# Values by the SyncE queue in fp32 and cast on GpSimd, in a kernel of gated attention and channel mixing

## The chip, the cores and the metric

The kernel runs on one core of one Trainium2 chip. The metric is the device time of a run in microseconds (us), the median of several runs. A core has five engines that run side by side, each with its own program in a fixed order: TensorE (PE in the profile; its weight loads are PEld), VectorE (DVE), ScalarE (ACT), GpSimd (POOL) and SyncE (SP), which only starts transfers here. Engines wait for each other by semaphores. Transfers between the device's memory and the on-chip memory run on 16 DMA engines; here they are started from two queues, that of SyncE (q1 in the profile) and that of GpSimd (q0).

## The reference

Queries, keys and values have 4 batches, 8 heads, 768 positions and 64 columns, in fp32. Keys are cut into 12 blocks of 64. A gate picks for each query the three best blocks by the product with the block's mean key, and its own block; attention is taken over these, causally. The result goes through a token mixing and a channel mixing:

```
k_rep = k.reshape(B, H, n_blocks, block, D).mean(axis=3)
gate_scores = np.einsum('bhsd,bhnd->bhsn', q, k_rep)      # masked causally by block
top_idx = np.argsort(gate_scores, axis=-1)[..., -top_k:]
...
scores = scale * np.matmul(q, k.transpose(0, 1, 3, 2))    # masked by chosen blocks and causally
attn = softmax(scores)
x = np.matmul(attn, v)                                    # heads side by side: 768 x 512 a batch
...
h = np.maximum(xt @ w_tok1, 0.0) @ w_tok2                 # xt: x turned
u = x + h.transpose(0, 2, 1)
out = u + np.maximum(u @ w_ch1, 0.0) @ w_ch2
```

## The kernel before

**The unit of work is a pair of heads**, 16 in all, four to a batch, numbered 0 to 15. For each pair the keys and then the queries are loaded in fp32 as tiles `kl` and `ql` of 128 partitions x 768 (`load_qk`, line 306, issued at line 313 in two halves, one a head, on the SyncE queue). TensorE turns each tile (`transposes`, line 358, names `tkl` and `tql`), ScalarE brings the result out of the accumulation memory (`evac_t`, line 367, `kt` and `qt`), and GpSimd casts it to fp16 head by head (`cast`, line 374, `KA` and `QA`; for pair 0 ScalarE does it). VectorE sums the keys by block (`ksum`, line 387), TensorE multiplies with the queries (`gate`, line 405), VectorE takes the top values (line 463) and makes the mask rows, which are put beside the queries (`put_mask`, line 499), so that the scores (line 513) come out masked. Pairs 0 to 5 are gated one by one, later ones in groups of two or four.

**Attention.** For each of a pair's two heads there are three groups of scores, three exponentials on ScalarE (line 526), for all pairs but the first a multiply of the diagonal blocks with a triangle on VectorE (`diag`, line 533), then 21 matmuls with the values (`av`, line 545) and the division by the sum (lines 553 and 564).

**Values.** The product needs them in fp16, with a column of ones behind the 64, in one of six buffers `V16`. `load_v` (line 316) fetches a pair's values with one transfer from GpSimd's queue (line 320), which casts fp32 to fp16 under way. A buffer can be filled again when the products of six pairs before are done.

**Weights.** Ten transfers on the same GpSimd queue (lines 706 to 711), also cast under way.

**Mixing.** Token mixing (lines 576 to 621) needs a batch's four pairs. Channel mixing (lines 657 and 678) is the larger part of TensorE's work; a batch's channel mixing is spread between the attention of later pairs, and the last is done alone at the end.

**What sets the order.** The kernel writes each engine's program out by hand. Before anything is issued, Python code makes a list of operations (`Op`: engine, time it occupies the engine, time until the result, what it depends on, priority, and for transfers a size) and runs a small model of the chip over it (`plan`, line 109). The model takes at each step the operation that can start soonest, by priority among those that are close; the order that comes out is the order of issue on every engine. SyncE loads are taken strictly by priority (line 155), while stores (kind SPO) go in where they come. `transfers` (line 80) models the two queues: where both have work they share the rate, with 60 to 90% for GpSimd's queue according to the size. Two of its habits matter here:
- A dependence in this list that isn't one of data orders the plan only. On the chip an engine waits for data and buffers, and otherwise for its own turn. The loop at line 831 ties each value load to the query transposes of a pair in this manner.
- Where nothing else is ready in the first 46 us of the plan, TensorE gets stand-in matmuls on a tile `warm` (line 695); their results are not used.

Pair i is prepared at priority `pre`, ahead of its attention at 10 i, by 25 for the first four pairs and by 10 later (with 5 more for groups); its key load has priority `pre - 12` and its query load 0.1 more (line 727). The value load (line 752) has `vpre + 2`.

Of the kernel before, what the change touches and what calls it, by code (L numbers as in the profile page):

```python
# [9 lines left out]
FP = mybir.dt.float32  # L10
# [18 lines left out]
R = 5  # L29
NBN = 4  # L30
# [9 lines left out]
def QACT(i):  # L40
    return i < 1


GATE = {2: 700, 3: 700, 4: 730}
GROUPED = [[0], [1], [2], [3], [4], [5], [6, 7], [8, 9, 10, 11], [12, 13, 14, 15]]
WAIT = [("kt", 3, 1), ("kt", 3, 1), ("qt", 3, 1), ("qt", 3, 1), ("qt", 4, 1), ("qt", 4, 1),
# [172 lines left out]
def kernel(  # L219
# [11 lines left out]
    nc = tc.nc  # L231
    B, H, S, D = q.shape
    NB = S // 64
    NJ = S // 128
# [12 lines left out]

    pairs = [(b, h) for b in range(B) for h in range(0, H, 2)]
    NP = len(pairs)
    RINGS = dict(big=2, bank=3, av=1, ql=3, kl=3, qt=4, kt=2, gs=1, gt=1, gm=1, m8=1, bn=NBN, e0=3, e1=3, e2=3, rc=2,  # L250
                 x16=2, h1=2, u=2, uT=2, h2=1, ob=3)

    def sb(tag, shape, dt, name):
        return sp.tile(shape, dt, tag=tag, bufs=RINGS[tag], name=name)

    def ps(tag, shape, name, dt=FP):
        if tag == "big":
            return pp.tile([128, 1024], FP, tag=tag, bufs=RINGS[tag], name=name)
        return pp.tile(shape, dt, tag=tag, bufs=RINGS[tag], name=name)


    avp = pp.tile([128, 512], FP, tag="av", bufs=1, name="avp")
    V16 = [sp.tile([128, 2, NJ, 65], F16, tag=f"V{r}", name=f"V{r}") for r in range(R + 1)]
# [23 lines left out]
    T = {}  # L287
# [3 lines left out]
    def op(eng, occ, rec, deps, prio, fn, takes=(), size=0):  # L291
        o = Op(eng, occ, rec, deps, prio, fn, takes, size)
        ops.append(o)
        return o

    def pe(occ, deps, prio, fn, takes=(), tail=170):
        return op("PE", occ, occ + tail, deps, prio, fn, takes)

    def act(cols, deps, prio, fn, takes=()):
        return op("ACT", 70 + cols * 0.833, 173 + cols * 0.833, deps, prio, fn, takes)  # L300
# [5 lines left out]
    def load_qk(i, t32, src):  # L306
        b, h = pairs[i]

        def f():
            t = sb(t32, [128, NJ, 2 * D], FP, f"{t32}_{i}")  # L310
            T[t32, i] = t
            for g in range(2):
                nc.sync.dma_start(out=t[:, :, D * g:D * g + D], in_=src[b, h + g].rearrange("(j p) d -> p j d", p=128))  # L313
        return f

    def load_v(i):
        b, h = pairs[i]

        def f():
            nc.gpsimd.dma_start(out=V16[i % (R + 1)].rearrange("p g j d -> p (g j) d")[:, :, 0:D],  # L320
                                in_=v[b, h:h + 2].rearrange("g (j p) d -> p (g j) d", p=128))
        return f


    def load_gate_consts():
        nc.sync.dma_start(out=gown, in_=consts["gown"])
# [25 lines left out]
    def transposes(t32, i):  # L352
        def f():
            p = ps("big", None, f"t{t32}")
            T["tr", t32, i] = p
            t = T[t32, i]
            for j in range(NJ):
                nc.tensor.transpose(out=p[:, 128 * j:128 * j + 128], in_=t[:, j, :], identity=ident32)  # L358
        return f
# [161 lines left out]
    def expo(i, x, g):  # L521
        def f():
            width = GROUPS[g][0]
            e = sp.tile([128, 1024 if g < 2 else 640], F16, tag=f"e{g}", bufs=RINGS[f"e{g}"], name=f"e{g}_{i}_{x}")
            T["e", i, x, g] = e
# [23 lines left out]
    def recip(i, x):  # L549
        def f():  # L550
            rc = sp.tile([128, NJ, 1], FP, tag="rc", bufs=RINGS["rc"], name="rc")
            T["rc", i, x] = rc
            nc.vector.reciprocal(out=rc.rearrange("p n o -> p (n o)"),
                                 in_=T["aps", i, x][:, :, 64:65].rearrange("p n o -> p (n o)"))
# [143 lines left out]
    O = {}  # L698
# [15 lines left out]
    def prepare(i):  # L714
        b, h = pairs[i]
        gi = [n for n, G in enumerate(GROUPED) if i in G][0]
        i0 = GROUPED[gi][0]
        pre = 10.0 * (i0 - (AHEAD if i < FIRST else LATER)) + 2.5 * (i - i0) - (0 if len(GROUPED[gi]) == 1 else EXTRA)
        vpre = 10.0 * (i - (AHEAD if i < FIRST else LATER))
        old = i - R  # L720

        def last_scores(x):
            return [O.get(("sc", old, x, g)) for g in range(3)]

        for t32, src, off in (("kl", k, 0), ("ql", q, 0.1)):
            bf = Buf(t32)
            O[t32, i] = op("SP", 950, 0, [], pre - 12 + off, load_qk(i, t32, src), [bf], size=1750)
            big = Buf("big")
            O["tr", t32, i] = pe(660, [O[t32, i]], pre + off, transposes(t32, i), [big], tail=320)
            bf.users.append(O["tr", t32, i])  # L730
            name = "kt" if t32 == "kl" else "qt"
            tb = Buf(name)
            O[name, i] = act(768, [O["tr", t32, i]],
                             pre + 0.5 + off, evac_t(t32, i), [tb])
            big.users.append(O[name, i])
            dst = KA if name == "kt" else QA
            for x in range(2):
                occ = 770
                if QACT(i):
                    O["cast", name, i, x] = act(768, [O[name, i]] + last_scores(x), pre + 0.9 + 0.2 * x + off, cast_act(dst, name, i, x))  # L740
                    tb.users.append(O["cast", name, i, x])
                    continue
                O["cast", name, i, x] = op("POOL", occ, occ + 55, [O[name, i]] + last_scores(x), pre + 4 + off,
                                           cast(dst, name, i, x))
                tb.users.append(O["cast", name, i, x])
            if name == "kt":
                O["ksum", i] = dve(870, [O["kt", i]], pre + 1, ksum(i))
                tb.users.append(O["ksum", i])
                O["kcopy", i] = dve(200, [O["ksum", i], O.get(("gate", old))], pre + 1, kcopy(i))
            else:  # L750
                qb = tb
        O["v", i] = op("POOL", 1060, 0, [O.get(("av", i - R - 1, x)) for x in range(2)], vpre + 2, load_v(i), size=1350)
        n = len(GROUPED[gi])
        O["qb", i] = qb
        if i == GROUPED[gi][-1]:
            G = GROUPED[gi]
            if n == 1:
                gb = Buf("bank")
                O["gate", i] = gate_op = pe(1120, [O["kcopy", i], O["qt", i]], pre + 2, gate(i), [gb])
            else:  # L760
                tbig = Buf("big")
                gate_op = pe(GATE[n], [O["kcopy", m] for m in G] + [O["qt", m] for m in G], pre + 2, gate_t(gi), [tbig])
                for m in G:
                    O["gate", m] = gate_op
                gtb = Buf("gt")
                ge = act(S - 128, [gate_op], pre + 2.1, gate_e(gi), [gtb])
                tbig.users.append(ge)
                gb = Buf("big")
                gback = pe(550, [ge], pre + 2.2, gate_b(gi), [gb])
                gtb.users.append(gback)  # L770
            for m in G:
                O["qb", m].users.append(gate_op)
            gs = Buf("gs")
            O["gm", gi] = dve(75 + 125 * n, [gate_op] if n == 1 else [gback, own_op], pre + 3, gm(gi), [gs])
            gb.users.append(O["gm", gi])
            tops = [dve(720, [O["gm", gi]], pre + 3, top(gi, s)) if s == 0 else None for s in range(n)]
            for s in range(1, n):
                tops[s] = dve(720, [tops[0]], pre + 3, top(gi, s))
            O["lt", gi] = dve(75 + 125 * n, tops, pre + 3, below(gi))
            O["bias", gi] = dve((75 + 125 * n) if n == 4 else 200 * n, [O["lt", gi], O.get(("mask", gi - NBN))] + ([own_op] if n == 4 else []), pre + 3, bias(gi))  # L780
            gs.users += [O["bias", gi]]
            O["lt", gi].two = O["bias", gi].two = True
            mb = Buf("bank")
            O["mask", gi] = pe(280, [O["bias", gi]], pre + 4, mask(gi), [mb])
            for s, m in enumerate(G):
                for x in range(2):
                    O["put", m, x] = dve(410, [O["mask", gi]] + [O.get(("sc", m - R, x, g)) for g in range(3)],
                                         pre + 4, put_mask(gi, s, x))
                    mb.users.append(O["put", m, x])
# [38 lines left out]
        for i in G:  # L828
            attend(i)

    for i, d in enumerate((1, 2, 2, 3, 3, 4, 4, 5, 6, 7, 8, 9, 10, 11, 12, 13)):
        O["v", i].deps.append(O["tr", "ql", d])
    own_op.deps.append(O["cast", "qt", 4, 1])
    for x in range(2):
        O["cast", "kt", 0, x].deps.append(O["qt", 0])
# [80 lines left out]
    kernel_plan.update(ops=O)  # L916
    order, span = plan(ops, RINGS)

# [65 lines left out]
```

The softmax here doesn't subtract the row's maximum and nothing guards it: scores larger than these inputs give would overflow.

## Time and profile before

| | |
|---|---|
| time, median of 3 runs | 266.84 us (266.03 to 267.7) |
| span of the profiled run | 265.2 us |
| TensorE clock granted | 0.998 |
| key loads: 32 transfers of 192 KB, issue to landing | 5.8 us median |
| query loads: 32 transfers of 192 KB | 5.5 us |
| value loads: 16 transfers of 192 KB (fp16 as written) | 8.3 us |
| weight loads: 8 of 384 KB for the channel mixing | 12.2 us |
| packets' time on q1 (SyncE), share of 16 engines | 38.6% for 21.33 MB |
| packets' time on q0 (GpSimd), share of 16 engines | 27.1% for 7.08 MB |

How to read the lines further on. In a table by stage each row has the stretch and its length in us, then the busy time and number of instructions of each engine, the granted clock, the DMA share (it can go over 1, since packets of two queues overlap on an engine) and GB/s. In a group of instructions the columns are the line, the engine, the operation, the tiles written and read, their shapes, the count, the busy time in us, the mean in ns, and the idle time of the engine ahead of them with what ended it. In the list of waits a row gives who waited, for whom, the sum in us, how many times, and sometimes the longest. In the list in order of time and in the chain of waits the first two numbers are the start and the length in us; a bracket at the end is the idle time just before. A busy TensorE isn't TensorE at its peak, because the ends of its instructions are modelled.

### The profile page before, as it was taken

What the parts mean: (1) busy time and instruction counts of PE and PEld (TensorE: products, weight loads), DVE (VectorE), ACT (ScalarE), POOL (GpSimd) and SP (SyncE); (2) the same over time, 40 slices, a digit from 0 to 9 for tenths busy, and PEclk for the clock granted to TensorE, in tenths of its full rate; (3) what the DMA queues carried; (4) which work ended last, traced back from release to release, by engine and by line L of the source; (5) the groups of instructions that cost most, each with busy time, mean ns of one, the idle gap of its engine ahead of it and who ended that gap; (6) DMA issues with size and microseconds to landing.
All of it is one profiled execution on the core that took longest, in us unless ns stands there. A gap on an engine that the chain in (4) does not pass through costs nothing.

```text
span 265.2 us, 5842 instructions
## 1 busy us (share of the span) xinstructions
PE 256.0 (97%) x2304; PEld 166.3 (63%) x2304; DVE 158.9 (60%) x536; ACT 145.3 (55%) x195; POOL 79.9 (30%) x112
## 2 busy tenths in 40 slices
PE   7889999999997999999999999999999999999994
PEld 7877888895765767455666566655455544456443
DVE  4668869896976569986557975493243253333222
ACT  3757898677796966458873699860034400044000
POOL 8494819849446645225420000000000000000000
PEclk9999999999999999999999999999999999999999
DMA  8999999999996999059511000009220025310032
GB/s 169 203 189 197 173 179 208 196 187 194 192 155 134 210 205 159 36 60 174 69 45 41 1 2 0 2 0 189 90 79 2 0 48 150 121 40 0 2 141 97
DMA packets 91322, 28.77 MB, mean 109 GB/s; under 512 B 84896, under 2 KB 87840, under 8 KB 91296
## 3 DMA queue, kind: packets, MB, share of 16 engines
q1 hardware_dynamic: 63232, 21.33, 38.6%
q0 software_dynamic: 28064, 7.08, 27.1%
q8 instruction: 18, 0.29, 0.5%
q14 instruction: 8, 0.07, 0.1%
HBM read 26.83 MB, written 6.29 MB: 125 GB/s over the span
## 4 chain that ended last, share of the span: by engine, by line
PE 84%; DVE 7%; SPq 2%; DMA 2%; ACT 1%; issue 1%; POOL 1%; DVEq 0%; ACTq 0%
PE c L657 23%; PE c L678 23%; PE sps L513 13%; PE avp L545 7%; PE ups L588 3%; PE tql L358 3%; PE tkl L358 2%; SPq L313 2%; DMA kl<-in_k_dram 2%; PE tok L576 2%; PE gps L405 2%; DVE m L463 1%; DVE kst L387 1%; PE gtp L415 1%; DVE QA L499 1%; PE tok L607 1%
## 5 line engine op out<-in xcount | busy, mean ns | idle before, releaser
L526 ACT ACTIVATE e<-sps 128x1024 f16<-128x1024 f32 (+1 forms) x96 | 84.3, 920 | 17.5 <-PE sps L513 14.0
L657 PE MATMUL c<-uT,wc 128*128 128x256 f16 (+1 forms) x384 | 69.1, 326 | 0.0
L678 PE MATMUL c<-wc,h 128*128 128x512 f16 (+2 forms) x300 | 65.6, 370 | 0.0
L667 ACT ACTIVATE h<-c 128x512 f16<-128x512 f32 x48 | 28.7, 598 | 61.1 <-PE c L657 42.9
L657 PEld LDWEIGHTS <-wc 128*128 128x128 f16 x384 | 36.5, 98 | 23.0 <-issue 0.2
L513 PE MATMUL sps<-QA,KA 88*128 88x512 f16 (+3 forms) x256 | 50.1, 305 | 0.0
L678 PEld LDWEIGHTS <-h 128*128 128x128 f16 x300 | 28.7, 98 | 30.6 <-issue 1.0
L533 DVE TENSOR_TENSOR e<-e,m 128x256 f16<-128x256 f16 x90 | 29.7, 337 | 14.5 <-ACT e L526 13.9
L374 POOL CAST KA<-kt 64x768 f16<-64x768 f32 x30 | 24.6, 821 | 45.1 <-ACT kt L367 28.0
L669 DVE TENSOR_SCALAR h<-c 128x256 f16<-128x256 f32 x48 | 20.3, 422 | 26.8 <-PE c L657 26.4
L686 DVE TENSOR_TENSOR ob<-u,c 128x512 f32<-128x512 f16 (+2 forms) x25 | 16.5, 664 | 32.2 <-PE c L678 32.1
L513 PEld LDWEIGHTS <-KA 88*128 88x128 f16 x256 | 23.1, 99 | 17.0 <-issue 0.7
L374 POOL CAST QA<-qt 64x768 f16<-64x768 f32 x30 | 25.5, 850 | 6.5 <-ACT qt L367 5.1
L545 PEld LDWEIGHTS <-e 128*128 128x128 f16 x672 | 25.4, 97 | 2.8
L545 PE MATMUL avp<-V,e 128*128 128x65 f16 x672 | 26.7, 193 | 0.0
L367 ACT COPY kt<-tkl 128x768 f32<-128x768 f32 x16 | 12.8, 798 | 12.8 <-PE tkl L358 7.2
L387 DVE TENSOR_REDUCE kst<-kt 128x12 f32<-128x768 f32 x16 | 15.2, 950 | 6.3 <-ACT kt L367 6.0
L564 DVE TENSOR_TENSOR x<-avp,rc 128x384 f16<-128x384 f32 x32 | 17.8, 555 | 0.8
L320 POOL DMA_DIRECT2D V<-in_v_dram x16 | 16.5, 1033 | 5.6 <-PE avp L545 3.4
L367 ACT COPY qt<-tql 128x768 f32<-128x768 f32 x16 | 12.8, 801 | 5.0 <-PE tql L358 5.0
L499 DVE COPY QA<-bps 24x640 f16<-24x640 f16 x32 | 14.3, 480 | 2.1 <-PE bps L493 1.8
L358 PE MATMUL tkl<-id,kl 128*128 128x128 f32 x96 | 13.6, 277 | 1.9 <-DMA kl<-in_k_dram 1.9
(66 smaller groups left out, 212.5 us busy)
## 6 DMA issues: line engine op xcount, KB each, us to landing
kl<-in_k_dram SPq DMA_DIRECT2D x32, 192.0 KB, 5.8
ql<-in_q_dram SPq DMA_DIRECT2D x32, 192.0 KB, 5.5
out_dram<-ob SPq DMA_DIRECT2D x23, 256.0 KB, 2.0
V<-in_v_dram POOLq DMA_DIRECT2D x16, 192.0 KB, 8.3
wc<-in_moe_w_ch_dram POOLq DMA_DIRECT2D x8, 384.0 KB, 12.2
w<-in_moe_w_tok_dram POOLq DMA_DIRECT2D x2, 384.0 KB, 9.8
out_dram<-ob SPq DMA_DIRECT2D x1, 160.0 KB, 1.8
out_dram<-ob SPq DMA_DIRECT2D x1, 96.0 KB, 1.7
```

Source lines behind the costliest of these rows:

```text
L358: nc.tensor.transpose(out=p[:, 128 * j:128 * j + 128], in_=t[:, j, :], identity=ident32)
L367: nc.scalar.copy(out=t, in_=p[:, 0:S])
L374: nc.gpsimd.tensor_copy(out=to, in_=src)
L387: nc.vector.tensor_reduce(out=kst, in_=kt.rearrange("p (n w) -> p n w", w=64), axis=AX.X, op=ALU.add)
L513: nc.tensor.matmul(out=p[:, off + a:off + a + n], lhsT=KA[i % R][x][0:MK, 128 * kk:128 * kk + 128], rhs=QA[i % R][x][0:MK, q0 + a:q0 + a + ...
L526: nc.scalar.activation(out=e[:, 0:width], in_=T["sps", i, x, g][:, 0:width], func=AF.Exp, scale=scale)
L533: nc.vector.tensor_tensor(out=d, in0=d, in1=m0.rearrange("p (a b) -> p a b", a=1).broadcast_to([128, 2, 128]), op=ALU.mult)
L545: nc.tensor.matmul(out=p[:, jq, :], lhsT=T["e", i, x, g][:, o:o + 128], rhs=V16[i % (R + 1)][:, x, kk, :], start=(kk == 0), stop=(kk == jq))
L657: nc.tensor.matmul(out=p, lhsT=wc1_16[:, cc, 128 * fc:128 * fc + 128], rhs=T["uT", b][:, cc, a // 128:e // 128, :], start=(cc == 0), stop= ...
L667: nc.scalar.activation(out=T["h2", b][:, fc, a:e], in_=T["c1", b, fc, n], func=AF.Relu)
L669: nc.vector.tensor_scalar(out=T["h2", b][:, fc, a:e], in0=T["c1", b, fc, n], scalar1=0.0, scalar2=None, op0=ALU.max)
L678: nc.tensor.matmul(out=T["c2", b, j, lo], lhsT=T["h2", b][:, fc, 128 * j:128 * j + 128], rhs=wc2_16[:, fc, lo:hi], start=(fc == 0), stop=( ...
```

## The change

Values no longer come through GpSimd's queue with a cast under way. They are loaded as fp32 by the SyncE queue into one of two new buffers `v32` (128 x 768 fp32), and GpSimd casts them from there into `V16` with an instruction. Where the loads stand among the key and query loads is written out in a list `VAT`, one priority for each pair: the values of pair 0 after the queries of pair 1, those of pair 1 after the queries of pair 2, those of 2 and 3 after the queries of pair 3, those of 4 and 5 after the queries of the same pair, 6 and 7 together after the queries of 7, and from pair 8 on each behind the queries of its pair. The cast stands in GpSimd's plan where the load stood, and waits for the load and for the products that free the buffer; a `v32` buffer is free again when its cast is done. The loop that tied the value loads to query transposes goes. What is left on GpSimd's queue is the ten weight loads. It is meant to keep the values from competing with keys and queries at times that the plan doesn't know, and to take them off the queue on which the weights wait.

```diff
+VAT = [-26.8, -16.8, -6.9, -6.8, 18.2, 28.2, 36.0, 36.1, 53.2, 55.7, 58.2, 60.7, 93.2, 95.7, 98.2, 100.7]
...
-    RINGS = dict(big=2, bank=3, av=1, ql=3, kl=3, qt=4, kt=2, gs=1, gt=1, gm=1, m8=1, bn=NBN, e0=3, e1=3, e2=3, rc=2,
+    RINGS = dict(big=2, bank=3, av=1, ql=3, kl=3, qt=4, kt=2, v32=2, gs=1, gt=1, gm=1, m8=1, bn=NBN, e0=3, e1=3, e2=3, rc=2,
                  x16=2, h1=2, u=2, uT=2, h2=1, ob=3)
...
         b, h = pairs[i]
 
         def f():
-            nc.gpsimd.dma_start(out=V16[i % (R + 1)].rearrange("p g j d -> p (g j) d")[:, :, 0:D],
-                                in_=v[b, h:h + 2].rearrange("g (j p) d -> p (g j) d", p=128))
-        return f
-
+            t = sb("v32", [128, 2 * NJ, D], FP, f"v32_{i}")
+            T["v32", i] = t
+            nc.sync.dma_start(out=t, in_=v[b, h:h + 2].rearrange("g (j p) d -> p (g j) d", p=128))
+        return f
+
+    def cast_v(i):
+        return lambda: nc.gpsimd.tensor_copy(out=V16[i % (R + 1)].rearrange("p g j d -> p (g j) d")[:, :, 0:D], in_=T["v32", i])
...
-        O["v", i] = op("POOL", 1060, 0, [O.get(("av", i - R - 1, x)) for x in range(2)], vpre + 2, load_v(i), size=1350)
+        vb = Buf("v32")
+        load = op("SP", 700, 0, [], VAT[i], load_v(i), [vb], size=1750)
+        O["v", i] = op("POOL", 820, 870, [load] + [O.get(("av", i - R - 1, x)) for x in range(2)], vpre + 2, cast_v(i))
+        vb.users.append(O["v", i])
...
-    for i, d in enumerate((1, 2, 2, 3, 3, 4, 4, 5, 6, 7, 8, 9, 10, 11, 12, 13)):
-        O["v", i].deps.append(O["tr", "ql", d])
     own_op.deps.append(O["cast", "qt", 4, 1])
```

## The prediction

> **What bounds the kernel now.** I read the totals of the page first, then the table by stage, then the stand-in matmuls alone, then the waits of TensorE, and last the chain and the groups. Totals, busy us and share of the span:
>
> ```profile
> PE 256.0 (97%) x2304; PEld 166.3 (63%) x2304; DVE 158.9 (60%) x536; ACT 145.3 (55%) x195; POOL 79.9 (30%) x112
> ```
>
> TensorE is the bound, with GpSimd (POOL) far from it. So an edit is worth only what it takes out of TensorE's time without useful work. The stages (length, then busy us and count of TensorE, its weight loads, VectorE, ScalarE and GpSimd, clock, DMA share, GB/s):
>
> ```profile
> 5.00:35.00 30.00, 28.02 (x350) 23.51 (x349) 21.08 (x88) 22.24 (x28) 19.71 (x24) 1.00 1.39 194
> 35.00:80.00 45.00, 44.77 (x547) 34.83 (x546) 37.33 (x138) 36.04 (x49) 28.66 (x38) 1.00 1.41 186
> 80.00:86.00 6.00, 4.25 (x48) 3.28 (x47) 4.02 (x10) 3.72 (x5) 4.46 (x6) 1.00 0.67 134
> 86.00:146.00 60.00, 59.52 (x554) 37.36 (x553) 43.63 (x176) 39.72 (x51) 23.04 (x27) 1.00 0.66 111
> ```
>
> The same table for line 695 alone, the stand-in matmuls that are issued where nothing else is ready:
>
> ```profile
> 5.00:35.00 30.00, 7.41 (x102) 6.26 (x102) 1.00 1.39 194
> 35.00:80.00 45.00, 0.00 (x0) 0.00 (x0) 1.00 1.41 186
> ```
>
> From 5 to 35 us TensorE idles 1.98 us and runs 102 stand-ins. The chain has 15 of them in 0.80 us, 0.053 us each; their busy time overlaps, so they cost 102 x 0.053 = 5.4 us. After 35 us there are none: the channel mixing of an earlier batch fills every gap. Idle time after that is 0.23, 1.75 and 0.48 us in the three stages. All that any edit of the loads can win is about 5.4 + 2.0 + 2.5 = 9.9 us, of which 7.4 lies before 35 us.
>
> Where the idle time lies, and the start of the chain:
>
> ```profile
> PE tkl L358 <- DMA kl<-in_k_dram: 1.9, 3, 1.1
> 82.22 0.84 PE L358 MATMUL tkl<-id,kl 128*128 128x128 f32 x6 [0.61 <-DMA kl<-in_k_dram]
> 85.50 0.85 PE L358 MATMUL tql<-id,ql 128*128 128x128 f32 x6 [1.14 <-ACT h L667]
> ...
> 7.63 5.70 DMA kl<-in_k_dram
> 13.33 0.14 issue
> 13.47 0.85 PE tkl L358 x6
> ```
>
> Two places count. At 13.47 the transposes of the third key tile come 1.07 us late. Behind them, in TensorE's fixed order, stand the first scores (14.15), though their mask rows were written by 12.89. At 82 to 86 us two transposes wait, 0.61 and 1.14 us; the second is put down to ScalarE, but as scores and output use other buffers I read it as the query load that follows in the queue.
>
> ```profile
> L320 POOL DMA_DIRECT2D V<-in_v_dram x16 | 16.5, 1033 | 5.6 <-PE avp L545 3.4 <-PE sps L513 2.2
> L374 POOL CAST QA<-qt 64x768 f16<-64x768 f32 x30 | 25.5, 850 | 6.5 <-ACT qt L367 5.1
> L533 DVE TENSOR_TENSOR e<-e,m 128x256 f16<-128x256 f16 x90 | 29.7, 337 | 14.5 <-ACT e L526 13.9
> 6.99 1.18 POOL L320 DMA_DIRECT2D V<-in_v_dram  x1
> ```
>
> The first of these is what is removed, the second prices what is added, the third is who can be disturbed, and the last is the cause of the late key tile: the first value load starts at 6.99. The planner is told to hold it until the query transposes of pair 1 (10.32), but that is an entry in its list and no wait on the chip, so the load runs 3.3 us sooner than the order was made for.
>
> **What the skill says.** (1) "DMA: Bandwidth & Descriptors", section "Issuing engines are not separate DMA queues": all queues share the same 16 engines, and changing queue saves only issue time. The trace agrees on the sharing: with no value load under way, a key or query tile of 1536 packets took 1.7 to 1.9 us from first packet to last; the tile of 9.1 to 12.4 us, beside the first value load (9.8 to 13.3), took 3.3. (2) Same page, "SWDGE vs HWDGE vs iDMA": a cast inside a DMA is only to be had from GpSimd's queue; so the move forces the cast instruction. (3) "SBUF — State Buffer", "Who interferes with whom": a VectorE instruction with two SBUF inputs contends with a GpSimd instruction that reads SBUF. The trace agrees: of the 90 diagonal multiplies (line 533), 19 overlap a GpSimd cast or copy and take 527 ns in the mean, 71 do not and take 287.
>
> **The change, part by part.**
>
> *GpSimd.* Removed: 16 issues x 1.033 = 16.5 us. Added: 16 casts of 128x768. No row shows 128 partitions; a 64x768 cast takes 0.821 to 0.850, and a 24x768 copy of line 333 takes 0.818, so the number of partitions hardly matters: 16 x 0.83 = 13.3 us (if it scaled with partitions, 26). Net -3.2 us on an engine that is 30% busy: worth nothing by itself. But a DMA issue did not read SBUF and a cast does: casts and copies on GpSimd go from 69 to 85. By proportion 19 x 16/69 = 4.4 more multiplies overlap, x 0.24 us = 1.1 us of VectorE, spread over 16 pairs while VectorE is 70 to 83% busy. I charge 0.3 us, between 0 (filled by other work) and 1.1.
>
> *The transfers.* From the packet records: a value load is 1536 packets of 32 ns on GpSimd's queue against 18 ns (alone) to 24 ns (contended) for the same 256 source bytes on the SyncE queue. Over 16 engines that is 3.1 against 1.7 to 2.3 us per load; for the 12 loads ahead of 85 us, 9 to 16 us of engine time less. Against it: with both queues active the engines overlap them (shares of 1.4 above), so part of that saving was never wall time. Over 28 to 84 us GpSimd's queue never ran dry, because values stood among the weights, and key and query tiles took up to 7 to 8 us each. With only 10 weight loads there (22.7 us of engine time) I estimate the eleventh key tile 3 to 4 us earlier. That removes most of the waits at 82 to 86: -1.4 of 1.75 us.
>
> *The first tiles.* The SyncE order becomes keys and queries of pairs 0 and 1, values 0, keys and queries 2, values 1, then pair 3. Queries 1 end at 9.2. Values 0 then take 9.2 to 11.0, keys 2 11.0 to 12.8, plus the 1.0 us seen between last packet and start of the transposes (12.4 to 13.47): 13.8 against 13.47. Queries 2: 15.6, as now. Keys 3 at about 19.3 are used at 22.4 now, so nothing waits. What changes is the order: the planner now has values 0 ahead of keys 2 on one queue, as the chip will, so the first scores (ready at about 13.0) need not stand behind a late transpose. Scores at about 13.1 instead of 14.15, and the gate of pair 1 (16.31 now, its sums ready at 14.24, standing behind the queries' transposes) up to 1.5 us sooner. ScalarE, near 100% busy from 26 to 37 us, starts its exponentials that much sooner, and stand-ins vanish by as much: -1.5 us, between +0.4 (same order, tile later) and -3.
>
> *New waits.* Each value load waits for one of two fp32 buffers, so for the cast two pairs earlier; behind it on SyncE stand the next keys. Load 7 waits for cast 5, load 10 for cast 8, load 12 for cast 10 (now those value loads are issued at 40.4, 58.2 and 66.9). SyncE in turn issues the key and query tiles next to them at about 46, 75 and 87 us, so each buffer is free by then: 0 for the forecast. The output stores stand behind all of it on SyncE, but begin at 111 us. A cast of values waits for the product five to six pairs back, as the load did (3.4 us once): same place in GpSimd's order, no new cost. Small gaps elsewhere (0.23 + 0.48): -0.4 with loads earlier.
>
> Sum: 0.3 - 1.4 - 1.5 - 0.4 = -3.0; 266.8 - 3.0 = 263.8 us.
>
> **Rivals.** A, *the start moves more*: of the 7.4 us without work before 35 us up to 4 vanish, since with queue and plan agreeing all orders up to pair 3 fit: 1.4 + 4 + 0.4 = 5.8, 261 us. For: 5.4 us of stand-ins; against: ScalarE 22.2 of 30 and VectorE 21.1 of 30 us busy there, so other chains close up. B, *hidden anyway*: the order at the start stays, keys 2 are 0.3 us later, the waits at 82 us go in part but VectorE's 0.3 to 1.1 us come back: 266.2. For: TensorE is filled after 35 us whatever the loads do. C, *the SyncE queue jams*: a value load waits for its buffer while keys stand behind it, or 16 more loads on one queue no longer overlap with the second. Keys of pairs 8 to 11 then come 3 to 6 us late, and with the wait of 82 us grown by that: 270. For: SyncE already takes up to 7 us for one tile's two issues at 68 us; against: the buffer dates above.
>
> **How the numbers follow.** Forecast 0.40, A 0.18, B 0.24, C 0.18. Over 1% faster is below 264.2: three quarters of the forecast case and A, 0.30 + 0.18 = 0.48. Within 1%: the rest of the forecast and B, 0.34. Slower: C, 0.18. The range from 260.0 to 268.0 holds the forecast and B, nearly all of A and the mild part of C.
>
> **What would show it.** Right: value packets at 18 to 24 ns; casts at about 0.83 us; the first scores before 13.5 us and before the third key transposes; fewer than 102 stand-ins; no idle stretch of TensorE over 0.5 us at 80 to 86; overlapped multiplies in the low twenties. Wrong: SyncE idle on a GpSimd cast with late key transposes behind it; stand-ins unchanged or more; casts near 1.6 us; idle TensorE time at a new place between 40 and 110 us.

## The result, and the profile after

The changed kernel takes 276.49 us (median of 4 runs, 274.1 to 278.36) beside 267.27 us of the kernel before (4 runs, 266.03 to 267.71): a ratio of 1.0323, with an interval of 1.0238 to 1.0408. It is 9.2 us slower by the medians (8.6 us without the run of 278.36 us, which was of a slower kind and is left out of the ratio), where 3.0 us less were forecast. The profiled execution has a span of 275.0 us.

The totals of the page after (busy us, share of the span, instructions):

```profile
PE 261.0 (95%) x2328; PEld 169.2 (62%) x2328; DVE 162.8 (59%) x536; ACT 145.5 (53%) x195; POOL 77.3 (28%) x112
```

TensorE is busy for 5 us more although its work is the same, and GpSimd for 2.6 us less, as planned. The table by stage says where (length, then busy us and count of TensorE, weight loads, VectorE, ScalarE, GpSimd, clock, DMA share, GB/s):

```profile
5.00:35.00 30.00, 28.28 (x366) 24.20 (x366) 20.50 (x85) 21.01 (x26) 18.83 (x24) 1.00 1.15 210
35.00:80.00 45.00, 37.81 (x431) 29.38 (x427) 29.69 (x93) 27.78 (x38) 26.84 (x37) 0.89 1.09 200
80.00:86.00 6.00, 6.00 (x62) 4.04 (x60) 5.51 (x35) 4.64 (x7) 0.83 (x1) 1.00 1.11 219
86.00:146.00 60.00, 59.60 (x567) 38.23 (x566) 46.68 (x144) 43.15 (x55) 26.83 (x32) 1.00 0.64 131
```

The loss lies in the second stage. Before, TensorE idled there for 0.23 us and ran 547 matmuls at full clock; now it idles for 7.19 us, runs 431, and the mean clock is 0.89. The other stages are as full as before or fuller. Which waits these are is seen in TensorE's timeline from 58 to 75 us (start, us, in brackets the idle time before and what ended it):

```profile
58.94 0.83 PE L625 MATMUL ups<-h,w 128*128 128x128 f16 x12
...
62.64 1.05 PE L362 MATMUL tql<-id,ql 128*128 128x128 f32 x6 [2.87 <-DMA ql<-in_q_dram]
67.66 1.51 PE L362 MATMUL tkl<-id,kl 128*128 128x128 f32 x6 [3.96 <-DMA kl<-in_k_dram]
...
70.89 1.91 PE L661 MATMUL c<-uT,wc 128*128 128x512 f16 x4
```

TensorE stands still for 2.87 us for the queries of pair 7 and for 3.96 us for the keys of pair 8. From 63.1 to 73.3 us its clock is at half, and the transposes between the waits take 1.05 to 1.51 us instead of 0.85. The chain of waits at that place leads to the load of the keys and from there to SyncE's queue:

```profile
59.79 3.37 SPq L314
63.16 0.05 issue
63.21 4.31 DMA kl<-in_k_dram
67.52 0.14 issue
67.66 1.51 PE tkl L362 x6
```

I give the landing of a load as the trace has it, in us, and beside it the time at which the kernel's own planner expected it when it wrote the order down.

| tile | landed before | landed after | the plan after expected |
|---|---|---|---|
| queries 2 | 15.49 | 16.64 | |
| queries 3 | 20.03 | 24.56 | |
| queries 6 | 45.26 | 53.94 | |
| keys 7 | 49.74 | 55.57 | |
| queries 7 | 56.91 | 62.51 | 49.3 |
| keys 8 | 62.25 | 67.52 | 52.4 |
| queries 8 | 67.74 | 69.31 | |
| keys 9 | 74.59 | 72.83 | |
| keys 10 | 82.09 | 82.68 | |

From queries 6 to keys 8 the tiles come 5 to 9 us later than before, and queries 7 and keys 8 come 13 and 15 us later than planned. Both columns turn out to matter. In the kernel before, keys 8 were planned for 51.8 us and also came late, at 62.2 us, but the order used them only at a planned 66.5 us, on the chip at 69.93 and without a wait (TensorE's timeline of the kernel before):

```profile
69.93 0.87 PE L358 MATMUL tkl<-id,kl 128*128 128x128 f32 x6
```

The order of the changed kernel uses them at a planned 57.4 us.

Why they come late is seen in the queues. From 36 to 60 us, the DMA view of each kernel (packets, MB written, time of their packets as a share of 16 engines), first before:

```profile
q0 software_dynamic: 7281, 2.92, 97.6%
q1 hardware_dynamic: 6477, 1.62, 44.4%
```

and after:

```profile
q0 software_dynamic: 1399, 2.47, 59.6%
q1 hardware_dynamic: 8222, 2.07, 43.2%
```

q1 is SyncE's queue, q0 GpSimd's. A key, query or value load is 1536 packets. Counted in such loads, SyncE's queue moved 4.1 of them before while 4.0 value loads went through GpSimd's queue among the weights: 8.1 in 24 us. After, SyncE's queue has to take all three kinds and moves 5.2. Its packets are cheaper than those of the casting loads were (21 ns in the mean over the whole kernel, against 32), but it gets no larger part of the engines. Where no weights run, the same queue moves 0.50 to 0.55 loads per us; beside the weights it moves 0.22, about 40%.

Counted in bytes written, nothing was lost: the two lines give 4.54 MB in the 24 us before and 4.54 MB after, and over the whole second stage the tables have 186 and 200 GB/s. But a value load that is cast under way writes 192 KB, and one in fp32 384 KB. At 0.19 MB per us the eight value loads of pairs 0 to 7 would then take about 8 us more (an estimate from these figures), which is near the 5 to 9 us above. Whether the limit is in bytes written or in how the queues share the engines isn't separated by any run here.

SyncE's own timeline shows it held up (start, us, issues):

```profile
32.22 11.46 SPq L314 DMA_DIRECT2D kl<-in_k_dram  x2
43.78 2.07 SPq L314 DMA_DIRECT2D ql<-in_q_dram  x2
```

The two issues of one key tile, that of pair 6, hold SyncE for 11.46 us, 8.47 of them for the first half. Its buffer had been free since the transposes of keys 3 (they start at 21.81), so I read this as a full queue; no run tests that reading.

The parts of the change itself, from the groups and the issues of the page after:

```profile
L327 POOL CAST V<-v 128x768 f16<-128x768 f32 x16 | 13.4, 835 | 30.9 <-DMA v<-in_v_dram 19.7
L537 DVE TENSOR_TENSOR e<-e,m 128x256 f16<-128x256 f16 x90 | 32.4, 371 | 14.4 <-ACT e L530 13.6
v<-in_v_dram SPq DMA_DIRECT2D x16, 384.0 KB, 5.6
```

A cast takes 835 ns, and GpSimd stands idle for 19.7 us ahead of casts whose values have not landed. The diagonal multiplies cost 2.7 us more than before.

### The profile page after: what moved, and what is told of

Read it like the earlier page. It is cut to its first block, busy times and chain, and to the rows that moved or that the text cites. A ratio compares the mean times of both kernels' runs of the same rounds, so it can differ in the third digit from the quotient of the medians.

```text
span 275.0 us, 5913 instructions
## 1 busy us (share of the span) xinstructions
PE 261.0 (95%) x2328; PEld 169.2 (62%) x2328; DVE 162.8 (59%) x536; ACT 145.5 (53%) x195; POOL 77.3 (28%) x112
## 4 chain that ended last, share of the span: by engine, by line
PE 80%; DVE 6%; DMA 5%; SPq 5%; issue 1%; ACT 1%; DVEq 0%; ACTq 0%
PE c L661 23%; PE c L682 22%; PE sps L517 12%; PE avp L549 7%; SPq L314 4%; DMA ql<-in_q_dram 4%; PE tql L362 3%; PE ups L592 2%; PE tkl L362 2%; PE tok L580 2%; DMA kl<-in_k_dram 2%; PE gtp L419 1%; DVE QA L503 1%; PE gps L409 1%; DVE m L467 1%
## 5 line engine op out<-in xcount | busy, mean ns | idle before, releaser
L661 PE MATMUL c<-uT,wc 128*128 128x256 f16 (+1 forms) x384 | 69.3, 328 | 0.0
L537 DVE TENSOR_TENSOR e<-e,m 128x256 f16<-128x256 f16 x90 | 32.4, 371 | 14.4 <-ACT e L530 13.6
L517 PEld LDWEIGHTS <-KA 88*128 88x128 f16 x256 | 22.4, 98 | 18.1 <-issue 2.7
L327 POOL CAST V<-v 128x768 f16<-128x768 f32 x16 | 13.4, 835 | 30.9 <-DMA v<-in_v_dram 19.7
L362 PE MATMUL tql<-id,ql 128*128 128x128 f32 x96 | 14.3, 288 | 4.2 <-DMA ql<-in_q_dram 4.2
L362 PE MATMUL tkl<-id,kl 128*128 128x128 f32 x96 | 14.2, 287 | 4.0 <-DMA kl<-in_k_dram 4.0
```

The costliest lines, as they stand in the source:

```text
L517: nc.tensor.matmul(out=p[:, off + a:off + a + n], lhsT=KA[i % R][x][0:MK, 128 * kk:128 * kk + 128], rhs=QA[i % R][x][0:MK, q0 + a:q0 + a + ...
L537: nc.vector.tensor_tensor(out=d, in0=d, in1=m0.rearrange("p (a b) -> p a b", a=1).broadcast_to([128, 2, 128]), op=ALU.mult)
L661: nc.tensor.matmul(out=p, lhsT=wc1_16[:, cc, 128 * fc:128 * fc + 128], rhs=T["uT", b][:, cc, a // 128:e // 128, :], start=(cc == 0), stop= ...
```

## The experiments

Two theories stood at the start. Theory 1: the 16 value loads in SyncE's queue delay the keys and queries. Theory 2: the casts on GpSimd do it, through VectorE or through what waits behind them. A third came up as the runs went on: the order that the planner wrote is made for landings that don't happen. The ratios are to the kernel before, on the same chip.

**e1: the loads of values 4 to 7 left out**.

```
 def f():                                  # load_v
+    if 4 <= i < 8:
+        T["v32", i] = T["v32", i - 2]
+        return
```

> The changed kernel with its order kept and the transfers of the values of pairs 4 to 7 left out (their casts read the buffers of pairs 2 and 3 again). Theory 1 (the values stand in SyncE's queue among keys and queries, and while the weights run on the other queue this one gets the smaller part): queries 7 and keys 8 arrive at least 7 us sooner, both waits of TensorE (2.87 and 3.96 us at 60 to 68 us) and the clock drop after them go: 264 to 268 us. Theory 2 (the casts on GpSimd and their contention with VectorE cost the time): the casts are all still there, so 274 to 277 us.

268.68 us, ratio 1.0097 (1.0062 to 1.0131): some 2.4 us are left of the loss, as the kernel before took 266.3 us beside it, with all casts in place. Queries 7 land at 53.40 and keys 8 at 55.99. TensorE's waits by releaser (us, number, longest):

```profile
PE tql L365 <- DMA ql<-in_q_dram: 1.7, 2, 1.1
PE tkl L365 <- DMA kl<-in_k_dram: 0.8, 1, 0.8
```

against 4.2 and 4.0 us of the changed kernel. So four transfers in that queue are enough for most of the loss. One thing more changes: casts that needn't wait let the last two weight loads start at 62.4 instead of 69.3 us.

**e2: the casts of values 6 to 15 left out**, with the loads kept.

```
 def cast_v(i):
+    if i >= 6:
+        return lambda: None
```

> The changed kernel with its order kept and the ten casts of values of pairs 6 to 15 left out (the products use the values of earlier pairs), all transfers kept. Theory 1 (SyncE's queue): the waits for queries 7 and keys 8 stay within 0.5 us of 2.87 and 3.96, 273 to 277 us. Theory 2 (casts): 8.3 us of GpSimd and the waits on it fall away, 266 to 271 us.

280.29 us, ratio 1.0535 (1.0492 to 1.0579): slower than the changed kernel, which neither theory had. TensorE's timeline:

```profile
67.73 1.52 PE L364 MATMUL tkl<-id,kl 128*128 128x128 f32 x6 [7.36 <-DMA kl<-in_k_dram]
```

One wait of 7.36 us stands in place of the two of 2.87 and 3.96 us: queries 7 land at 57.00 here, and keys 8 at 67.59, as in the changed kernel. What comes later than there are queries 8 (72.30 against 69.31, with a wait of 2.55 us) and keys 9 (75.72 against 72.83). The reason stands on GpSimd. Its issue of the last two weight loads, in the timeline of GpSimd in e2:

```profile
61.97 1.52 POOL L717 DMA_DIRECT2D wc<-in_moe_w_ch_dram  x2
```

and in the changed kernel:

```profile
69.34 1.52 POOL L715 DMA_DIRECT2D wc<-in_moe_w_ch_dram  x2
```

Without casts that wait for values, these loads start 7.4 us sooner, and then queries 8 and the end of keys 8 travel beside them. So leaving the casts out wins nothing, and the waiting casts had even held the competition back. As the weights moved with them, this alone doesn't clear the casts; e1 and e5, with all casts in place and little or no loss, do, and theory 2 falls. The price that theory 1 had left out is the weights beside the queue.

**e3: 50 and 70 stand-ins ahead of the two late transposes**, to keep the clock up.

```
+ahead = {id(O["tr", "ql", 7]): 50, id(O["tr", "kl", 8]): 70}
 for o in order:
+    for n in range(ahead.get(id(o), 0)):
+        dummy(n)()
```

> The changed kernel with 50 stand-in matmuls ahead of the transposes of queries 7 and 70 ahead of those of keys 8, in the time in which TensorE waits (about 2.7 and 3.8 us of stand-ins). If the clock drop to about half at 64 to 73 us comes from TensorE having stood still: clock stays at 1.0, and the time falls by 2.5 to 3.5 us to 272.5 to 274. If the drop has another cause: 276 to 277 us.

276.57 us, ratio 1.0363 (1.0291 to 1.0435), the same as the changed kernel. One stretch of 5 us, first of the changed kernel:

```profile
65.00:70.00 5.00, 2.34 (x14) 2.31 (x15) 0.15 (x1) 0.66 (x1) 3.85 (x5) 0.50 1.16 223
```

then of e3:

```profile
65.00:70.00 5.00, 3.45 (x55) 3.27 (x53) 1.71 (x7) 0.80 (x1) 4.49 (x6) 1.00 0.92 200
```

And TensorE's timeline of e3 after that:

```profile
69.78 0.85 PE L362 MATMUL tql<-id,ql 128*128 128x128 f32 x6 [1.55 <-DMA ql<-in_q_dram]
74.87 0.85 PE L362 MATMUL tkl<-id,kl 128*128 128x128 f32 x6 [2.23 <-DMA kl<-in_k_dram]
```

The clock stays at 1.00 and nothing is won: faster work arrives sooner at the next late load and waits there. The test isn't quite clean, since queries 7 landed at 56.27 in this execution, so that the first 50 stand-ins filled a wait that wasn't there; keys 8 landed at 66.91, about as the 70 stand-ins ended. I had counted the slow clock as part of the loss; it is a sign of the wait, and the landings set the time.

**e4: the loads of values 6 and 7 moved behind queries 8**, the rest of the order kept.

```
+late = [O["vload", 6], O["vload", 7]]
+order = [o for o in order if o not in late]
+at = order.index(O["ql", 8]) + 1
+order[at:at] = late
```

> The changed kernel with the loads of values 6 and 7 moved on SyncE from before keys 8 to behind queries 8, every other order kept. Theory 1: keys 8 land two loads, about 3.6 us, sooner, the wait for them falls from 3.96 to under 0.8 us, the wait for queries 7 stays at 2.9, the clock drop is shorter: 270 to 273 us, unless the casts of values 6 and 7, now later, hold up the query casts behind them by as much. Theory 2 (casts): no change, 275 to 278 us.

278.52 us, ratio 1.0468 (1.0429 to 1.0507); missed. Keys 8 land at 64.27, 3.3 us sooner, but the waits only move:

```profile
64.36 1.51 PE L362 MATMUL tkl<-id,kl 128*128 128x128 f32 x6 [3.73 <-DMA kl<-in_k_dram]
...
74.04 1.51 PE L362 MATMUL tkl<-id,kl 128*128 128x128 f32 x6 [3.01 <-DMA kl<-in_k_dram]
```

Values 6 and 7 now stand ahead of keys 9, which land at 73.91 instead of 72.83. GpSimd stands idle for 12.22 us for the values of pair 6 and issues the last weights at 72.5, and these run beside keys 10 (landed at 83.08).

**e5: the planner keeps the backlog.** The planner models the queues' rates, but two of its lines drop every transfer that was due over 2 us ago. With the transfer goes the work it leaves in the queue, so later loads are believed early. Without these lines it plans the changed kernel anew:

```
 for o, d in transfers(moves).items():
     done[id(o)] = max(done.get(id(o), 0.0), d)
-now = min(free.values())
-moves = [(a, o) for a, o in moves if done[id(o)] > now - 2000]
```

> The changed kernel with one line of the planner taken out: the one that forgets transfers already due to be done, so that the plan loses the queue's backlog. Its plan then has keys 8 landing at 72.7 us instead of 52.4 (on the chip 67.5), and all orders are made anew from that. Theory 1a (the transfers are slow, but it is TensorE's fixed order, made for loads 13 to 15 us earlier, that turns this into waits): TensorE's waits for loads fall below 1 us in all, 264 to 269 us. Theory 1b (between 47 and 75 us there is nothing else to do than wait for the loads, whatever the order): the idle time comes back as stand-ins or other waits, 273 to 278 us.

267.25 us (20 runs), ratio 1.0025 (1.0004 to 1.0047). The loss is gone, with all 16 loads and casts in place and, up to 90 us, SyncE's issues in the same order as in the changed kernel. TensorE's waits for loads in e5:

```profile
PE tql L360 <- DMA ql<-in_q_dram: 1.1, 2, 0.7
```

and its second stage:

```profile
35.00:80.00 45.00, 43.70 (x514) 33.13 (x514) 35.39 (x129) 32.97 (x46) 24.19 (x34) 1.00 1.06 204
```

The transfers are about as slow as in the changed kernel: keys 8 land at 68.37, later than there, and 26 loads are through SyncE's queue at 68 us in both. But now the plan expects keys 8 at 72.7, and TensorE does other work first. In its timeline the queries of pair 7 and the keys of pair 8 are turned without a wait:

```profile
66.20 0.82 PE L360 MATMUL tql<-id,ql 128*128 128x128 f32 x6
...
75.74 0.82 PE L360 MATMUL tkl<-id,kl 128*128 128x128 f32 x6
```

The new plan also moves weight loads (two start at 56.9 instead of 53.2, the last two at 64.7 instead of 69.3), and queries 7 land at 57.39 instead of 62.51. That isn't what removes their wait: at 66.20 the landing of the changed kernel would have been in time too. So the slow queue alone costs nothing here; it costs when the order of the work counts on a fast one.

**e6: the last four weight loads later.** In the changed kernel they move on GpSimd behind the query cast of pair 9; **e7** does the same to the kernel before.

```
+late = W[6:10]
+order = [o for o in order if o not in late]
+at = order.index(O["cast", "qt", 9, 1]) + 1
+order[at:at] = late
```

> The changed kernel with every order kept but one: the four loads of the second channel weights on GpSimd come after the query cast of pair 9 (about 88 us) instead of at 53 and 69 us; nothing needs them before 110 us. Theory 1: without a second queue SyncE's queue runs at its full rate of a load in 1.8 us from 53 us on; queries 7 land 2 to 3 us sooner, keys 8 about 6 us sooner; the waits of 2.87 and 3.96 us fall below 1.5 us in all: 265 to 270 us. If the queue were slow by itself: the same waits, 274 to 278 us.

> The kernel before, with the same four weight loads moved behind the query cast of pair 9 (about 85 us) and nothing else. If keys and queries of pairs 7 to 11 are late there for the same reason: keys 10 land before 80 us, the waits of 0.6 and 1.1 us at 82 to 86 go, 263.5 to 265.5 us. If values on GpSimd's queue were the larger part: no change, 266 to 267 us.

e6: 273.41 us, ratio 1.0196 (1.0129 to 1.0263): about 3 us of the 9.2, less than I expected, and with an interval that overlaps that of the changed kernel. With the weights away, queries 7 land at 57.29 and keys 8 at 62.67, 4.9 us sooner, and TensorE waits 2.60 us for the latter, since the order still counts on 52.4. That the weights slow SyncE's queue is shown by the landings; moving them away isn't enough. e7: 274.4 us, ratio 1.0247 (1.0181 to 1.0312), where I expected no harm. The weights, now at 86.8 to 100.8 us, travel beside the tiles of pairs 13 and 14; queries 14 land at 107.74, and an order that was made without that waits:

```profile
107.87 1.51 PE L358 MATMUL tql<-id,ql 128*128 128x128 f32 x6 [3.36 <-DMA ql<-in_q_dram]
```

So the kernel before, too, is sensitive to a transfer that comes later than its order assumes.

**e8: values 0 to 3 alone by SyncE**, all others as before with their ties; planned with the two lines.

```
+def ON_SP(i):
+    return i < 4
```

> Half of the change: values of pairs 0 to 3 by SyncE with a cast, those of 4 to 15 by GpSimd's queue as before, tied in the plan as before. Theory 1: by 28 us both kernels have moved equally many loads, and no weights run before 30 us, so this half costs little: 265 to 269 us. Rival (the early values delay keys 2 and 3, and the delay is carried to the end): 270 to 274 us.

275.76 us, ratio 1.0304 (1.0226 to 1.0381); missed, the loss is nearly whole. The wait is of the same kind as in the changed kernel, though values 6 and 7 aren't in SyncE's queue:

```profile
65.10 1.51 PE L372 MATMUL tkl<-id,kl 128*128 128x128 f32 x6 [4.00 <-DMA kl<-in_k_dram]
```

So it isn't a matter of which values are in the queue at 50 us. Each new plan places its order anew against landings that it believes too early.

**e9: the kernel before, with the planner's two lines out** (edit as e5).

> The kernel before with the same planner line taken out as in the fifth experiment, values on GpSimd's queue. If both ways of loading values are about equal once the plan knows the backlog: 265 to 268 us, like the changed kernel with that line out (267.25). If the move itself costs something that the better plan only hid: 261 to 264.5 us here. If the old plan's optimism did the kernel before good: 269 us or more.

267.33 us (20 runs), ratio 1.0011 (0.9981 to 1.0042). The second stage:

```profile
35.00:80.00 45.00, 43.82 (x533) 33.66 (x529) 34.80 (x127) 32.57 (x46) 25.88 (x35) 1.00 1.30 189
```

With a plan that keeps the backlog, values through GpSimd's queue give 267.33 us and values through SyncE's 267.25 us, with ratios of 1.0025 and 1.0011 whose intervals overlap. The way that the values take is worth nothing that 20 runs can tell.

**e10: the kernel before with the lines out and a hopeful share of rates; e11: the changed kernel with the same.** With both queues at work the two now get 1.2 of the rate together.

```
-SHARE = ((3000.0, 0.8), (2000.0, 0.9), (0.0, 0.6))
+SHARE = ((3000.0, 0.85), (2000.0, 0.85), (0.0, 0.6))
...
-rate[False] = 1.0 - rate[True]
+rate[False] = 1.2 - rate[True]
```

> The kernel before with the planner's line out and its sharing set nearer to what the traces show (weights 0.85 of the rate, the other queue 0.35 beside them, so that two queues together move 1.2). Plan and chip then differ less for keys of pairs 7 to 11: waits for loads below 1 us, 263 to 266 us; if such waits weren't what bounds it: 266 to 268 us.

> The changed kernel with the planner's line out and the same sharing (0.85, 0.35). In the fifth experiment loads landed 4 to 10 us before the plan thought at 44 to 70 us; with this they should agree within 4 us. Theory 1a: no waits for loads over 1 us, 265 to 267.5 us. If that plan is now too hopeful again, keys 8 are waited for and the time is 270 us or more.

e10: 274.94 us, ratio 1.0252 (1.0167 to 1.0337); missed. An order that is too hopeful harms the kernel before in the way the change did:

```profile
62.93 1.20 PE L356 MATMUL tkl<-id,kl 128*128 128x128 f32 x6 [4.46 <-DMA kl<-in_k_dram]
```

e11: 270.48 us, ratio 1.0122 (1.0065 to 1.0178), with four waits for queries of 3.2 us in all. That is less lost than in e10 and more than in e5.

**e12: values 8 to 15 alone by SyncE, planned as e10; e15: the same values, planned as e5.**

```
+def ON_SP(i):
+    return i >= 8
```

> Values of pairs 8 to 15 by SyncE with a cast, those of 0 to 7 by GpSimd's queue as before, with the planner's line out and the sharing 0.85 and 0.35. While the weights run, values then stand in the favoured queue, and later on the even one. Theory 1: loads up to 60 us as in the kernel before, no waits over 1 us, 262.5 to 265.5 us, faster than both. If the gain is eaten by the eight casts or a new order: 266 to 269 us.

> Values of pairs 8 to 15 by SyncE with a cast, the others by GpSimd's queue, and the planner's line out with its sharing as it was (the pessimistic one, which did well in the fifth and ninth experiments). The twelfth experiment had the hopeful sharing and waited 8.7 us for one query tile. If hope in the plan was the trouble: no wait over 1.2 us, 263 to 268 us. If values by SyncE from pair 8 on are the trouble: 272 us or more.

e12: 273.77 to 279.69 us in four runs, too far apart for a ratio. e15: 268.5 us (8 runs), ratio 1.0077 (1.0035 to 1.0119). The longest wait of e12, in a run of 277.97 us:

```profile
69.35 1.51 PE L370 MATMUL tql<-id,ql 128*128 128x128 f32 x6 [8.72 <-DMA ql<-in_q_dram]
```

and those of e15:

```profile
PE tkl L370 <- DMA kl<-in_k_dram: 1.5, 2, 1.1
```

The same transfers with two plans are at least 3 us apart (273.77 is the quickest run of e12, 270.81 the slowest of e15). No mixture beats the kernel before.

**e13: the changed kernel, transfers in the same order on both queues, only the compute reordered by hand.** The transposes of queries 7, keys 8, queries 8 and keys 9, and what hangs on them, stand behind about 4.3 us of channel mixing.

```
+move = [("tr", "ql", 7), ("tr", "kl", 8), ("tr", "ql", 8), ("tr", "kl", 9), ...]
+at = order.index(O["ch1", 0, 2, 0]) + 1
+order[at:at] = move
```

> The changed kernel with its transfers in the same order on both queues. Only on TensorE, and with it on ScalarE, VectorE and GpSimd, the transposes of queries 7, keys 8, queries 8 and keys 9 and what hangs on them are put behind 4.3 us of channel mixing, scores, masks and products (about 4.6 us of work) that the plan had behind them. If the order makes the loss: this work fills as much of the 6.8 us of waits, less after-effects, 269 to 273 us. If the slow transfers make it, whatever the order: 275 to 278 us.

273.26 us, ratio 1.0257 (1.0231 to 1.0283), just above the range that I gave for the order. All four runs are quicker than the quickest of the changed kernel (273.96 against 274.1), and the median is 3.2 us lower, but the intervals of the ratios overlap, so how much the order alone won isn't settled. The waits:

```profile
PE tkl L362 <- DMA kl<-in_k_dram: 2.3, 2, 1.7
PE sps L517 <- DVE QA L503: 1.0, 1, 1.0
PE tql L362 <- DMA ql<-in_q_dram: 0.6, 1, 0.6
```

2.9 us for loads instead of 8.2, the clock at 1.0 up to the last microseconds, and a new wait of 1.0 us for mask rows. Queries 7 landed at 56.41 here, so the wait of 2.87 us for them would have been gone anyway; but e2 shows that TensorE then stands 7.36 us for keys 8, and here, where these land at 66.53, it doesn't stand for them at all. The waits thus support the third theory without any change to the planner. Why some 6 us remain to e5 was not looked into.

**e14: the kernel before without the loop that ties value loads to the transposes**, which the change also removes.

```
-for i, d in enumerate((1, 2, 2, 3, 3, 4, 4, 5, 6, 7, 8, 9, 10, 11, 12, 13)):
-    O["v", i].deps.append(O["tr", "ql", d])
```

> The kernel before without the loop that ties the value loads to query transposes in the plan, and nothing else of the change. If this tie is what holds values back from keys 2 and 3: the first value loads start no earlier on the chip (6.99 us already) but are planned so, 266 to 269 us. If the tie carries the before kernel's order through the weights' time: 272 us or more.

274.12 us, ratio 1.03 (1.0245 to 1.0355). The size is that of the change, the cause another one:

```profile
18.07 1.51 PE L358 MATMUL tkl<-id,kl 128*128 128x128 f32 x6 [3.60 <-DMA kl<-in_k_dram]
```

Value loads are issued at 3.84, 8.1 and 9.1 us and delay keys 2 to 17.9 us. The changed kernel has no such wait, since its planned places (VAT) do the loop's work. So the missing loop is not what made it slow, and similar times are no evidence of a similar cause.

## Why the prediction was wrong

*GpSimd: right.* Casts of 835 ns against 0.83 us forecast, GpSimd 2.6 us less busy against 3.2, and worth nothing.

*VectorE's charge: right in kind, too small in size.* 27 of the 90 diagonal multiplies overlap a cast or copy, against 19 before and about 23 forecast, and take 570 ns against 285 for the others: 2.7 us on the group against the 1.1 that I bounded it by. VectorE is not what TensorE waits for at 59 to 75 us.

*"The transfers" is the first step that failed: 1.4 us were to be won, and the late tiles are where the 9 us begin.* The prices per packet were right (median 18 ns), and so was the saving of the engines' time: from 36 to 60 us the shares of the two queues add up to 142% before and 103% after. The step from there to "the eleventh key tile 3 to 4 us earlier" was not: keys 10 land at 82.68 instead of 82.09. None of the saved time became time of arrival, as the bytes written per us stayed the same. I took GpSimd's queue for the one that held SyncE's back by its values, and expected SyncE to speed up once only weights were left there. It did, but only from 4.1 to 5.2 loads in 24 us (0.17 to 0.22 per us), while the 4.0 value loads that had travelled among the weights now had to find room in it. The Trainium skill, "DMA: Bandwidth & Descriptors", section "Issuing engines are not separate DMA queues", says that all queues end on the same 16 engines; I read from this that moving a load changes only what it costs to issue. For the end time of a plan that fits, e5 and e9 agree with it (267.25 and 267.33). For single tiles that reading is too short: with the values in SyncE's queue others landed 5 to 9 us later.

*"The first tiles": right in its mechanism, no gain.* The first scores start at 12.67 us and the gate of pair 1 is sooner by 2.0 us. Here are the first scores, and the queries of pair 3 later on:

```profile
12.67 0.38 PE L517 MATMUL sps<-QA,KA 88*128 88x512 f16 x1
...
24.70 0.84 PE L362 MATMUL tql<-id,ql 128*128 128x128 f32 x6 [0.84 <-DMA ql<-in_q_dram]
```

But I followed the queue only up to keys 3. Queries 3 stand behind values 0 to 2 (values 2 are issued at 16.64, ahead of queries 3 at 17.68, and not behind them, as the description of the change has it). They land 4.5 us later than before, and TensorE fills and waits. The table for line 699 alone, the stand-ins:

```profile
5.00:35.00 30.00, 8.59 (x124) 7.43 (x124) 1.00 1.15 210
35.00:80.00 45.00, 0.27 (x2) 0.19 (x2) 0.89 1.09 200
```

126 stand-ins instead of 102, at 0.053 us some 1.3 us more instead of 1.5 less.

*"New waits": zero for the buffers was about right, the step as a whole is the second that failed.* SyncE's waits put down to GpSimd ahead of value loads are 2.3 us in all, 1.0 at the longest, little against tiles that are 5 to 9 us late. But the step put new waits at zero, and TensorE idles 7.19 us from 35 to 80 us. What it left out is the order itself. I had even used one place where the planner's order and the chip disagreed (the first value load, 3.3 us sooner than planned). I did not ask how far the order trusts planned landings elsewhere, and what happens when the loads behind them slow down. The slack that keys 8 had before, 66.5 planned for use against 51.8 for landing, was what hid a landing 10 us late; the new plan left 5 us for one 15 us late.

*80 to 86 us:* no idle time, as foreseen, but only because all work had shifted.

*Rivals.* C had the symptom: keys of pair 8 late by 5.3 us, by loads on one queue that "no longer overlap with the second", and time past the range. Of its two reasons, the waiting for buffers didn't happen, and the lost overlap did (a DMA share of 1.43 before and 1.03 after, from 36 to 60 us), though not its later tiles: keys 9 come 1.8 us sooner and keys 10 0.6 us later. It was sized at 270, too low, as it added the lateness to one old wait and not to an order with two new ones.

*The signs named ahead.* Two of the signs of being wrong came true: more stand-ins than 102, and idle time of TensorE at a new place between 40 and 110 us.

How sure the cause is: e1 takes away four transfers, e5 takes away the error of the plan and keeps the transfers, and each brings back most or all of the loss; e9 says that the plan's repair is no gain by itself; e13 changes the order of the compute engines alone, and the wait for keys 8 goes. So this loss needs both, late tiles and an order that counts on early ones. The plans agree: the three that keep the backlog with the old sharing (e5, e9, e15) take 267 to 268.5 us whichever queue the values take; of those that forget it or share hopefully, the kernel before takes 267 us and all others (e8, e10, e11, e12, e14 and the changed kernel) take 270 us or more. An order that doesn't fit costs as much without the change (e7, e10, e14). Left open is whether the tiles are late because of the bytes that fp32 values write or because of how the 16 engines share beside the weights; no run here changes the size of a packet.

## What to carry to other kernels

Where a fixed order of work is laid out against a model of transfers, first compare the model's landing times with the trace's, before and for the changed load: a load that lands later than the order assumes stops the whole engine, while one that lands as late but is expected then costs nothing (276.49 against 267.25 us for the same loads). A queue's speed when alone doesn't tell its speed beside another with larger loads: read it from a stretch where both run, and count whole loads and bytes written per us over all queues, not ns per packet. When a wait is shifted by an edit rather than removed (e3, e4, e6), suspect what the waits have in common.

## What the runs showed of the hardware

SyncE's queue of 256-byte packets keeps 0.22 of 0.55 loads per us beside weight loads whose packets are larger (1024 to 3072 bytes as written), and a single issue of 192 KB then holds SyncE for up to 8.47 us. The two kernels write the same 4.54 MB from 36 to 60 us, though the packets' time differs by the shares of 142% and 103%.

The half clock came in stretches of 3.4, 6.8, 10.2 and 13.7 us. From 35 us on they came with waits of 2.6 us or more (2.60 in e6, 7.36 in e2); near 20 us e9 has one of 3.4 us with no wait over 1 us in the 10 us ahead of it. The Trainium skill, "TensorE: Matmul & The Clock Gate", Part 1, has a free-running window of about 3.4 us, and the lengths, all multiples of it, agree. What I had not expected is that it may cost nothing: with the clock kept up (e3) the time stayed at 276.57 us, since the next load was not there yet.

The multiplies that run beside a GpSimd cast take twice as long, 570 ns against 285, which fits what the Trainium skill says in "SBUF — State Buffer", "Who interferes with whom": a VectorE instruction with two SBUF inputs contends with a GpSimd instruction that reads SBUF.
